# Linear attention and a gated feed-forward layer on one core: attention of the next batch placed in pieces between the feed-forward matmuls

## Chip, core and metric

The kernel runs on one core of one Trainium2 chip. The core has five engines that run their own instruction streams and wait for each other by semaphores: TensorE (PE in the profile; PEld is its weight loading), VectorE (DVE), ScalarE (ACT), GpSimd (POOL, which here only issues loads and sets up constants) and SyncE (SP, which issues the stores). The metric is the device time of one execution in microseconds (us); lower is better.

## What is computed

Eight batches with 8 heads each, a sequence of 1024 and a head dimension of 64. K and V are first projected along the sequence to 64 rows by two fixed matrices E and F, so each head's score matrix is only 1024 x 64. The result of all heads, 8192 tokens of 512 features, goes through a feed-forward layer of width 1536 with a sigmoid gate.

```python
k_proj = np.einsum('ks,bhsd->bhkd', E, k)
v_proj = np.einsum('ks,bhsd->bhkd', F, v)
scores = scale * np.matmul(q, k_proj.transpose(0, 1, 3, 2))
scores = scores - np.max(scores, axis=-1, keepdims=True)
attn = np.exp(scores)
attn = attn / (np.sum(attn, axis=-1, keepdims=True) + 1e-09)
x = np.matmul(attn, v_proj)            # then heads side by side: (8192, 512)
gate = 1.0 / (1.0 + np.exp(-(x @ w_gate)))
val = x @ w_val
out = gate * val @ w_out
```

All inputs and the output are float32 in memory; loads convert to bfloat16 on the way, and the matmuls run in bfloat16 with float32 sums.

## The kernel before

The kernel has two stages, one after the other, with an instruction stream written out by hand for each engine (`pool_prog`, `dve_prog`, `pe_prog`, `act_prog`, `sync_prog`).

**Attention.** The loop runs over 32 pairs of heads (`NPAIR`, four per batch). For a pair, PE does these steps: `P1` projects K (L284) and V (L296), 16 matmuls of 64 columns each, the two heads on the two column halves of the PE array (`tile_position` (0, 0) and (0, 64)), so that their results stand in the upper and lower 64 partitions. `P2` transposes Q (L320, 16 transposes of 128 columns, in blocks of eight, first one head and then the other). `P34` makes the scores with the sequence on the partitions (L340). ACT takes the exponential (L524); no maximum is subtracted. DVE sums it along the 64 columns (L214), takes the reciprocal (L221) and multiplies (L226, `softmax_pair`). `P5` transposes the weights back (L357), DVE copies them out of PSUM (L204, L207), and `P6` multiplies by the projected V (L382). ACT copies the result to `xT` (L507, L511), which holds the feed-forward input of all batches, and does the copies of the transposed Q (L495, L498) and of the projections (L487). PE's order around a pair is P34(g), P5(g-1), P2(g+1), P1(g+1), P6(g-1).

**Feed-forward.** After all pairs, PE waits for the last `xT` and then runs over 16 blocks of 512 tokens. A block has 12 steps (`m`, 128 features of the inner width each): four matmuls for the gate (L454), four for the value (L465), each 128x128 by 512 columns. ACT takes the sigmoid of the gate out of PSUM (L541), DVE multiplies it by the value, also out of PSUM (L257), into `hT`. Gate and value banks and the sigmoid buffers are double. After the steps of a block come the output projections of the block before, `emit_outproj`: four tiles of 128 tokens, 12 matmuls each (L430). DVE copies each tile out (L245), SP stores it (L557) from one of two buffers.

**Loads.** POOL issues, in this order: E and F, then for each batch K, V and Q (L163, L166, L169) into two sets of buffers; the gate and value weights in three pieces each (L174, L177) come behind the loads of batch 5, the output weights (L180) last. From batch 2 on the issue waits until PE has read the buffers of two batches earlier. All these loads run in one DMA queue.

DVE's first operations make an identity matrix from two index tables (L188, L189, L191).

Of the kernel before, what the change touches and what calls it, by code (L numbers as in the profile page):

```python
# [6 lines left out]
AF = mybir.ActivationFunctionType  # L7
ALU = mybir.AluOpType
AX = mybir.AxisListType
# [4 lines left out]
P = 128  # L14
S = 1024
# [7 lines left out]
NSLOT = 2  # L23


def bass_linformer_attn__then__ffn_glu_sigmoid_kernel(
# [14 lines left out]
    assert H * DH == DM and H % 2 == 0  # L41
    NPAIR = B * (H // 2)
    PPB = H // 2
    NBLK = B * 2
    NTOT = NBLK * 4
    SCALE = 1.0 / (DH ** 0.5)

    with contextlib.ExitStack() as es:
        _cnt = [0]

        def sbuf(shape, dtype, name="sb"):
            _cnt[0] += 1
            return es.enter_context(nc.sbuf_tensor(f"{name}{_cnt[0]}", shape, dtype))

        def psum(shape, name="ps"):
            _cnt[0] += 1
            return es.enter_context(nc.psum_tensor(f"{name}{_cnt[0]}", shape, FP32))

        def sem():
            _cnt[0] += 1  # L60
            return es.enter_context(nc.semaphore(f"sem{_cnt[0]}"))

        iota_c_i = sbuf([P, P], I32)
        iota_r_i = sbuf([P, 1], I32)
        iota_c = sbuf([P, P], FP32)
        iota_r = sbuf([P, 1], FP32)
        ident = sbuf([P, P], BF16)
        Ebf = sbuf([KPJ, S], BF16)
        Fbf = sbuf([KPJ, S], BF16)
        Eperm = sbuf([KPJ, NT, P], BF16)  # L70
        Fperm = sbuf([KPJ, NT, P], BF16)
        ETp = sbuf([P, NT, KPJ], BF16)
        FTp = sbuf([P, NT, KPJ], BF16)

        Qb = [sbuf([P, H, NT * DH], BF16) for _ in range(NSLOT)]
        Kb = [sbuf([P, H, NT * DH], BF16) for _ in range(NSLOT)]
        Vb = [sbuf([P, H, NT * DH], BF16) for _ in range(NSLOT)]

        qTp = [sbuf([P, S], BF16) for _ in range(2)]
        kpvpSB = [sbuf([P, 128], BF16) for _ in range(3)]  # L80
        attnTp = [sbuf([P, S], BF16) for _ in range(2)]
        expb = [sbuf([P, 2, NT, KPJ], BF16) for _ in range(2)]
        attnN = [sbuf([P, 2, NT, KPJ], BF16) for _ in range(2)]
        rsb = [sbuf([P, 2 * NT], FP32) for _ in range(2)]
        rdb = [sbuf([P, 2 * NT], FP32) for _ in range(2)]

        xT = sbuf([P, NI, B * S], BF16)

        wG = sbuf([P, NI, DFF], BF16)
        wV = sbuf([P, NI, DFF], BF16)  # L90
        wO = sbuf([P, NF, DM], BF16)
        sig = [sbuf([P, 512], BF16) for _ in range(2)]
        hT = [sbuf([P, NF, 512], BF16) for _ in range(2)]
        ostage = [sbuf([P, DM], FP32) for _ in range(2)]

        pkv = psum([P, 512])
        pqbank = psum([P, 512])
        po1 = psum([P, 512])
        psc = [psum([P, 512]) for _ in range(2)]
        patbank = [psum([P, 512]) for _ in range(2)]  # L100
        po0 = psum([P, 512])
        pq = pqbank[:, :].bitcast(BF16)
        pat = [patbank[i][:, :].bitcast(BF16) for i in range(2)]
        pG = [pkv[:, 0:512], pqbank[:, 0:512]]
        pV = [po1[:, 0:512], psc[0][:, 0:512]]
        pO = [psc[1][:, 0:512], po0[:, 0:512]]

        sem_ef = sem()
        sem_q = [sem() for _ in range(NSLOT)]
        sem_k = [sem() for _ in range(NSLOT)]  # L110
        sem_v = [sem() for _ in range(NSLOT)]
        NWCH = 3
        sem_wg = [sem() for _ in range(NWCH)]
        sem_wv = [sem() for _ in range(NWCH)]
        sem_wo = sem()
        sem_out = [sem(), sem()]
        sem_init_iota = sem()
        sem_init_perm = sem()
        sem_init_pe = sem()
        sem_init_act = sem()  # L120
        sem_pe_kpvp = sem()
        sem_pe_qT = sem()
        sem_pe_scores = sem()
        sem_pe_trans = sem()
        sem_pe_out = sem()
        sem_act_qT = sem()
        sem_act_exp = sem()
        sem_act_xT = sem()
        sem_act_kpvp = sem()
        sem_dve_red = sem()  # L130
        sem_dve_rcp = sem()
        sem_dve_norm = sem()
        sem_dve_attnT = sem()
        sem_pe_gate = sem()
        sem_pe_val = sem()
        sem_pe_proj = sem()
        sem_act_sig = sem()
        sem_dve_h = sem()
        sem_dve_oevac = sem()

        out_v = out[:, :].rearrange("(x y) c -> y x c", y=NT)

        with nc.Block() as block:

            def pool_prog(gp):
                gp.iota(iota_c_i[:, :], [[1, P]], channel_multiplier=0)
                gp.iota(iota_r_i[:, :], [[1, 1]], channel_multiplier=1).then_inc(
                    sem_init_iota, 1
                )
                gp.dma_start(Ebf[:, :], E[:, :]).then_inc(sem_ef, 16)  # L150
                gp.dma_start(Fbf[:, :], F[:, :]).then_inc(sem_ef, 16)
                CW = DFF // NWCH
                wg_v = moe_w_gate.rearrange("(i p) f -> p i f", p=P)
# [439 lines left out]
```

## Time and profile before

| | us |
|---|---|
| median of 3 runs | 689.93 (689.55 to 691.05) |
| profiled execution, first to last instruction | 687.5 |
| first matmul of the attention stage on the projections | 17.85 |
| first weight load of the feed-forward stage | 185.53 |

The profiled execution has 2.4 us less span than the median of the timed runs: the span leaves out what lies before the first instruction and after the last. A group's row gives busy time, the mean duration of one instruction in ns, and the idle time of the engine just before with what ended it. Matmul durations hold the way through the array, so that those of a row of matmuls overlap; the rate is read from the starts. "PEclk" is the granted clock of TensorE as a share of full speed. A chain of waits goes back from the last instruction to what released each step.

### The profile page before, as it was taken

How to read it: one execution, taken by the hardware profiler on the slowest of the kernel's cores; microseconds unless marked ns; L12 is line 12 of the kernel's file. 1: busy time of each engine (PE TensorE's matmuls, PEld its weight loads, DVE VectorE, ACT ScalarE, POOL GpSimd, SP SyncE). 2: the span in 40 equal slices, each digit the busy share in tenths (PEclk: the TensorE clock that was granted, in tenths of full speed). 3: DMA queues.
4: the chain of work that ended last, by engine and by line, in shares of the span. 5: the costliest groups of instructions: out<-in, count | busy, mean ns of one | idle time of the engine just before them, and what ended most of it. 6: DMA issues, size and time to landing. Idle time of an engine off the chain costs nothing.

```text
span 687.5 us, 11735 instructions
## 1 busy us (share of the span) xinstructions
PE 603.9 (88%) x4961; PEld 311.4 (45%) x5008; DVE 286.7 (42%) x421; ACT 221.8 (32%) x420; POOL 29.1 (4%) x39
## 2 busy tenths in 40 slices
PE   0676666367599999999999999999999999999998
PEld 0555555255344444444444444444444444444443
DVE  1377777537433343433333343433333333334332
ACT  1377777357433131312212131312222131312220
POOL 4011141200000000000000000000000000000000
PEclk9999999779899999999999999999999999999999
DMA  9999999996000101010100101010100101010102
GB/s 143 207 165 177 184 176 207 207 207 102 2 0 1 51 11 62 0 62 15 47 31 31 47 17 61 1 61 1 62 31 33 47 15 62 1 61 1 61 16 107
DMA packets 39107, 47.67 MB, mean 69 GB/s; under 512 B 1552, under 2 KB 30736, under 8 KB 39056
## 3 DMA queue, kind: packets, MB, share of 16 engines
q0 software_dynamic: 29840, 30.15, 27.0%
q1 hardware_dynamic: 9216, 16.78, 6.5%
q8 instruction: 39, 0.64, 0.4%
q14 instruction: 12, 0.10, 0.0%
HBM read 60.29 MB, written 16.78 MB: 112 GB/s over the span
## 4 chain that ended last, share of the span: by engine, by line
PE 77%; DVE 11%; DMA 10%; issue 1%; POOL 1%; ACT 1%; POOLq 0%
PE ps L454 24%; PE ps L465 24%; PE ps L430 24%; DMA sb<-in_q_dram 10%; DVE sb L226 4%; DVE sb L214 4%; PE ps L357 3%; DVE sb L204 1%; DVE sb L207 1%; DVE sb L221 1%; PE ps L320 1%; POOL sb L163 0%; POOL sb L166 0%; PE ps L382 0%; PE ps L340 0%
## 5 line engine op out<-in xcount | busy, mean ns | idle before, releaser
L541 ACT ACTIVATE sb<-ps 128x512 bf16<-128x512 f32 x192 | 114.6, 597 | 361.9 <-PE ps L454 361.9
L257 DVE TENSOR_TENSOR sb<-sb,ps 128x512 bf16<-128x512 bf16 x192 | 132.1, 688 | 204.3 <-PE ps L465 204.3
L454 PE MATMUL ps<-sb 128*128 128x512 bf16 x751 | 195.6, 380 | 2.0 <-ACT sb L511 1.2
L465 PE MATMUL ps<-sb 128*128 128x512 bf16 x754 | 195.7, 380 | 0.7
L430 PE MATMUL ps<-sb 128*128 128x512 bf16 x752 | 167.2, 379 | 0.8
L454 PEld LDWEIGHTS ps<-sb 128*128 128x128 bf16 x768 | 75.2, 98 | 92.3 <-ACT sb L511 1.6
L465 PEld LDWEIGHTS ps<-sb 128*128 128x128 bf16 x768 | 75.4, 98 | 91.2 <-issue 1.1
L430 PEld LDWEIGHTS ps<-sb 128*128 128x128 bf16 x768 | 75.1, 98 | 90.6
L245 DVE COPY sb<-ps 128x512 f32<-128x512 f32 x64 | 44.3, 692 | 120.8 <-PE ps L430 118.6
L357 PE MATMUL ps<-sb 128*64 128x128 bf16 x512 | 30.2, 231 | 31.9 <-DVE sb L226 31.9
L214 DVE TENSOR_REDUCE sb<-sb 128x16 f32<-128x1024 bf16 x32 | 38.7, 1209 | 20.1 <-ACT sb L524 20.1
L320 PE MATMUL ps<-sb 128*64 128x128 bf16 x512 | 31.2, 235 | 16.3 <-DMA sb<-in_q_dram 16.3
L357 PEld LDWEIGHTS ps<-sb 128*64 128x64 bf16 x512 | 24.8, 115 | 36.1 <-DVE sb L226 36.0
L495 ACT ACTIVATE sb<-ps 128x512 bf16<-128x512 bf16 x32 | 19.1, 597 | 64.4 <-PE ps L320 64.4
L226 DVE TENSOR_TENSOR sb<-sb 128x1024 bf16<-128x1024 bf16 x32 | 39.2, 1225 | 1.1
L524 ACT ACTIVATE sb<-ps 128x512 bf16<-128x512 f32 x64 | 36.1, 646 | 1.5 <-PE ps L340 1.5
L320 PEld LDWEIGHTS ps<-sb 128*64 128x64 bf16 x512 | 25.7, 118 | 16.7 <-DMA sb<-in_q_dram 16.6
L204 DVE COPY sb<-ps 128x512 bf16<-128x512 bf16 x32 | 13.6, 424 | 46.4 <-PE ps L357 46.4
L284 PE MATMUL ps<-sb 128*64 128x64 bf16 x512 | 21.7, 203 | 9.4 <-DMA sb<-in_v_dram 9.4
L340 PE MATMUL ps<-sb 64*128 64x64 bf16 x512 | 18.5, 194 | 10.1 <-ACT sb L498 8.5
L340 PEld LDWEIGHTS ps<-sb 64*128 64x128 bf16 x512 | 15.0, 97 | 25.1 <-ACT sb L498 24.5
L382 PE MATMUL ps<-sb 64*64 64x512 bf16 x128 | 21.1, 411 | 1.7 <-DVE sb L207 1.7
(37 smaller groups left out, 187.4 us busy)
## 6 DMA issues: line engine op xcount, KB each, us to landing
out_dram<-sb SPq DMA_DIRECT2D x64, 256.0 KB, 2.0
sb<-in_k_dram POOLq DMA_DIRECT2D x8, 1024.0 KB, 9.7
sb<-in_v_dram POOLq DMA_DIRECT2D x8, 1024.0 KB, 14.2
sb<-in_q_dram POOLq DMA_DIRECT2D x8, 1024.0 KB, 18.3
sb<-in_moe_w_gate_dram POOLq DMA_DIRECT2D x3, 512.0 KB, 23.4
sb<-in_moe_w_val_dram POOLq DMA_DIRECT2D x3, 512.0 KB, 25.2
sb<-in_moe_w_out_dram POOLq DMA_DIRECT2D x1, 1536.0 KB, 36.5
sb<-in_E_dram POOLq DMA_DIRECT2D x1, 128.0 KB, 3.0
```

What stands on the lines that cost most here:

```text
L214: dv.tensor_reduce(rsb[ps][:, :], expb[ps][:, :, :, :].rearrange("p h t k -> p (h t) k"), AX.X, ALU.add,).then_inc(sem_dve_red, 1)
L226: dv.tensor_tensor(attnN[ps][:, :, :, :].rearrange("p h t k -> p (h t) k"), expb[ps][:, :, :, :].rearrange("p h t k -> p (h t) k"), bcast, ...
L245: dv.tensor_copy(ostage[T % 2][:, :], pO[T % 2][:, 0:512]).then_inc(sem_dve_oevac, 1)
L257: dv.tensor_tensor(hT[hslot][:, m, :], sig[M % 2][:, :], pV[M % 2][:, 0:512], ALU.mult).then_inc(sem_dve_h, 1)
L320: last = te.matmul(pq[ho : ho + 64, t * P : (t + 1) * P], Qb[sb][:, h, t * DH : (t + 1) * DH], ident[:, :], is_transpose=True, tile_positi ...
L340: last = te.matmul(psc[hl][:, t * KPJ : (t + 1) * KPJ], qTp[sp][ho : ho + 64, t * P : (t + 1) * P], kpvpSB[skv][ho : ho + 64, 0:64], tile_ ...
L357: last = te.matmul(pat[sa][ho : ho + 64, t * P : (t + 1) * P], attnN[sa][:, hl, t, :], ident[:, :], is_transpose=True, tile_position=(0, ho),)
L430: last = te.matmul(pO[T % 2][:, 0:512], hT[hslot][:, m, tt * P : (tt + 1) * P], wO[:, m, :], start=(m == 0), stop=(m == NF - 1),)
L454: last = te.matmul(pG[M % 2][:, 0:512], wG[:, i, m * P : (m + 1) * P], xT[:, i, c0 : c0 + 512], start=(i == 0), stop=(i == NI - 1),)
L465: last = te.matmul(pV[M % 2][:, 0:512], wV[:, i, m * P : (m + 1) * P], xT[:, i, c0 : c0 + 512], start=(i == 0), stop=(i == NI - 1),)
L524: ac.activation(expb[ps][:, hl, :, :].rearrange("p t k -> p (t k)"), psc[hl][:, :], AF.Exp, scale=SCALE,).then_inc(sem_act_exp, 1)
L541: ac.activation(sig[M % 2][:, :], pG[M % 2][:, 0:512], AF.Sigmoid).then_inc(sem_act_sig, 1)
```

## The change

The order of all work is now written by one program that records operations (`Plan.add`) with the data that each reads (`r`), writes (`w`) or holds alone (`x`, a PSUM bank), and then emits each engine's stream in the recorded order with the waits that follow (`Plan.emit`). There is one counting semaphore per engine; every operation on which another one depends increments its own engine's.

Attention of batch 0 runs first, alone. Then, for each batch b, the 24 feed-forward steps and the output tiles of the blocks before them form a list of slots (`slots`), 32 per batch (28 in the first), and the 25 pieces of attention of batch b+1 are placed between the slots, at most one behind each. An output tile follows every third step. `xT` has two buffers of one batch in place of one for all. Three PSUM banks (`PA`) serve attention in turn, two each serve gate and value, one the output tiles.

Attention itself changes. The projections (`kv`) run for four head pairs at once, 256 columns, the two column halves in turn; the projected K is transposed (`kt`) into a block-diagonal matrix of 128x128 per head pair (`kpBD`), and V is copied into another (`vpBD`). Q is transposed with the heads in turn (`qt`). Scores (`sc`) come out transposed: the 64 projected rows of both heads on the partitions, 512 tokens as columns. The exponential goes straight to `eT`, and its sums over the partitions are matmuls with a matrix of ones and zeros, four 32-column tiles in turn (`den`). DVE takes the reciprocal in four pieces of 128 columns (`rec`), splits it into a bfloat16 part and its remainder (`split`), one matmul with a selecting matrix spreads it over the partitions (`bc`), DVE multiplies, and one matmul per head pair and half sequence gives `xT` (`xo`).

The sigmoid becomes a hyperbolic tangent of half the gate; DVE adds one and multiplies by the value in one operation, and the factor of one half is applied where an output tile is copied out. The tangent is kept in float32, in three buffers; there are four output buffers.

The loads stand in the order E, F, K, V, Q of batch 0, the six gate and value pieces, K, V, Q of batch 1, the output weights, then batches 2 to 7. POOL also fills the constant matrices: four wide and sixteen small memsets and one more index table, between the loads of batch 0 and those of the weights. From the diff (helpers and constants cut; `...` where lines are left out):

```diff
-                for g in range(NPAIR + 1):
-                    if g < NPAIR:
-                        P34(g)
-                    if g >= 1:
-                        P5(g - 1)
-                    if g + 1 < NPAIR:
-                        P2(g + 1)
-                        P1(g + 1)
-                    if g >= 1:
-                        P6(g - 1)
-                te.wait_ge(sem_act_xT, 2 * NPAIR)
-                te.wait_ge(sem_act_kpvp, NPAIR)
-                te.wait_ge(sem_dve_attnT, 2 * NPAIR)
...
-                    ac.activation(sig[M % 2][:, :], pG[M % 2][:, 0:512], AF.Sigmoid).then_inc(
...
+class Plan:
...
+    def add(self, eng, fn, r=(), w=(), x=(), dma=None):
...
+        def dep(o, raw):
+            if o is op:
+                return
+            if o.eng == eng and o.dma is None:
+                if eng == "PE" or (eng != "POOL" and not raw):
+                    return
+            deps[id(o)] = o
...
+        for k in tuple(w) + tuple(x):
+            for o in self.writers.get(k, ()):
+                dep(o, False)
+            for o in self.readers.get(k, ()):
+                dep(o, False)
...
+                for op in mine:
+                    want = {}
+                    for o in op.deps:
+                        want[o.sem] = max(want.get(o.sem, 0), o.val)
+                    for s, v in want.items():
+                        if seen.get(s, 0) < v:
+                            e.wait_ge(sem(s), v)
+                            seen[s] = v
+                    inst = op.fn(e)
...
+        bank = [
+            es.enter_context(nc.psum_tensor(n, [P, 512], FP32))
+            for n in ("pG0", "pG1", "pV0", "pV1", "pO", "pA0", "pA1", "pA2")
+        ]
+        PG, PV, PO, PA = (0, 1), (2, 3), 4, (5, 6, 7)
...
+        def mm(b, o, lhsT, rhs, r, start=True, stop=True, tp=None, tr=False):
...
+                kw["start"], kw["stop"] = start, stop
+            return add("PE", lambda e: e.matmul(o, lhsT, rhs, **kw), r=r, x=[("bank", b)])
+        def act(o, i, r, w, b=None, func=AF.Copy, scale=1.0):
+            x = [] if b is None else [("bank", b)]
+            return add("ACT", lambda e: e.activation(o, i, func, scale=scale), r=r, w=w, x=x)
...
+        def next_bank():
+            b = PA[turn[0] % 3]
+            turn[0] += 1
+            return b
+        def attention(b):
+            s = b % 2
+            st = {}
+            def kv():
+                bk = next_bank()
+                for src, wt, c0, n in ((Kb[s], ET, 0, "K"), (Vb[s], FT, 256, "V")):
+                    sv = src[:, :, :].rearrange("p (r h) (t d) -> p h t r d", h=2, t=NT)
+                    for t in range(NT):
+                        for h in range(2):
+                            mm(
+                                bk,
+                                bank[bk][64 * h : 64 * h + 64, c0 : c0 + 256],
+                                wt[:, t, :],
+                                sv[:, h, t, :, :],
+                                [(n, s), ("ET" if n == "K" else "FT")],
                                 start=(t == 0),
                                 stop=(t == NT - 1),
+                                tp=(0, 64 * h),
                             )
+                act(kp[:, :, :], bank[bk][:, 0:256], [], ["kp"], b=bk)
+                for h in range(2):
+                    hh = slice(64 * h, 64 * h + 64)
+                    act(
+                        vpBD[hh, :, hh],
+                        bank[bk][hh, 256:512].rearrange("p (r d) -> p r d", r=NR),
+                        [],
+                        [f"vpBD{h}"],
+                        b=bk,
+                    )
+            def kt():
+                bk = next_bank()
+                ob = bank[bk][:, :].bitcast(BF16)
+                for r in range(NR):
+                    for h in range(2):
+                        mm(
+                            bk,
+                            ob[64 * h : 64 * h + 64, r * P : (r + 1) * P],
+                            kp[:, r, :],
+                            ident[:, :],
+                            ["kp", "ident"],
+                            tr=True,
+                            tp=(0, 64 * h),
+                        )
+                for h in range(2):
+                    hh = slice(64 * h, 64 * h + 64)
+                    act(
+                        kpBD[hh, :, hh],
+                        ob[hh, 0:512].rearrange("p (r c) -> p r c", r=NR)[:, :, hh],
+                        [],
+                        [f"kpBD{h}"],
+                        b=bk,
+                    )
+            def qt(r):
+                bk = next_bank()
+                ob = bank[bk][:, :].bitcast(BF16)
                 for t in range(NT):
+                    for h in range(2):
+                        mm(
+                            bk,
+                            ob[64 * h : 64 * h + 64, t * P : (t + 1) * P],
+                            Qb[s][:, 2 * r + h, t * DH : (t + 1) * DH],
+                            ident[:, :],
+                            [("Q", s), "ident"],
+                            tr=True,
+                            tp=(0, 64 * h),
+                        )
+                dve(lambda e: e.tensor_copy(qT[:, r, :], ob[:, :]), [], [("qT", r)], b=bk)
+            def sc(r):
+                for hf in range(2):
+                    bk = next_bank()
+                    mm(
+                        bk,
+                        bank[bk][:, :],
+                        kpBD[:, r, :],
+                        qT[:, r, hf * 512 : (hf + 1) * 512],
+                        ["kpBD0", "kpBD1", ("qT", r)],
                     )
+                    act(
+                        eT[:, r, hf, :],
+                        bank[bk][:, :],
+                        [],
+                        [("eT", r, hf)],
+                        b=bk,
+                        func=AF.Exp,
+                        scale=SCALE,
                     )
+            def den():
+                bk = next_bank()
+                st["den"] = bk
+                for rnd in range(2):
+                    for j in range(4):
+                        r, hf = 2 * rnd + j // 2, j % 2
+                        mm(
+                            bk,
+                            bank[bk][32 * j : 32 * j + 32, :],
+                            dsel[:, rnd, :],
+                            eT[:, r, hf, :],
+                            ["dsel", ("eT", r, hf)],
+                            start=(rnd == 0),
+                            stop=(rnd == 1),
+                            tp=(0, 32 * j),
+                        )
+            def rec(c):
+                bk = st["den"]
+                cc = slice(c * 128, (c + 1) * 128)
+                dve(
+                    lambda e: e.reciprocal(rden[:, cc], bank[bk][:, cc]),
+                    [],
+                    [("rden", c)],
+                    b=bk,
+                )
+            def split():
+                rd = [("rden", c) for c in range(4)]
+                dve(lambda e: e.tensor_copy(rhi[:, :], rden[:, :]), rd, ["rhi"])
+                dve(
+                    lambda e: e.scalar_tensor_tensor(
+                        rhl[:, :], rhi[:, :], negm[:, 0:1], rden[:, :], ALU.mult, ALU.add
+                    ),
+                    rd + ["rhi", "negm"],
+                    ["rhl"],
+                )
+            def bc(c):
+                r, hf = c // 2, c % 2
+                rnd, j = r // 2, 2 * (r % 2) + hf
+                bk = next_bank()
+                mm(bk, bank[bk][:, :], bsel[:, j, rnd, :], rhl[:, :], ["bsel", "rhl"])
+                dve(
+                    lambda e: e.tensor_tensor(
+                        aT[c % 2][:, :], eT[:, r, hf, :], bank[bk][:, :], ALU.mult
+                    ),
+                    [("eT", r, hf)],
+                    [("aT", c % 2)],
+                    b=bk,
+                )
+            def xo(c):
+                r, hf = c // 2, c % 2
+                bk = next_bank()
+                mm(
+                    bk,
+                    bank[bk][:, :],
+                    vpBD[:, r, :],
+                    aT[c % 2][:, :],
+                    ["vpBD0", "vpBD1", ("aT", c % 2)],
+                )
+                act(
+                    xT[s][:, r, hf * 512 : (hf + 1) * 512],
+                    bank[bk][:, :],
+                    [],
+                    [("xT", s, r, hf)],
+                    b=bk,
+                )
+            out = [kv, lambda: qt(0), kt, lambda: qt(1)]
+            out += [lambda: sc(0), lambda: qt(2), lambda: sc(1), lambda: qt(3)]
+            out += [lambda: sc(2), lambda: sc(3), den]
+            out += [lambda c=c: rec(c) for c in range(4)] + [split]
+            out += [lambda: bc(0)]
+            for c in range(1, 8):
+                out += [lambda c=c: (bc(c), xo(c - 1))]
+            out += [lambda: xo(7)]
+            return out
+        def mstep(blk, m):
+            s, hf = (blk // 2) % 2, blk % 2
+            M = blk * NF + m
+            j = m // (NF // NWCH)
+            for W, pb, n in ((wG, PG[M % 2], "wG"), (wV, PV[M % 2], "wV")):
+                for i in range(NI):
+                    mm(
+                        pb,
+                        bank[pb][:, :],
+                        W[:, i, m * P : (m + 1) * P],
+                        xT[s][:, i, hf * 512 : (hf + 1) * 512],
+                        [(n, j), ("xT", s, i, hf)],
+                        start=(i == 0),
+                        stop=(i == NI - 1),
                     )
+            sg = sig[M % 3]
+            act(
+                sg[:, :],
+                bank[PG[M % 2]][:, :],
+                [],
+                [("sig", M % 3)],
+                b=PG[M % 2],
+                func=AF.Tanh,
+                scale=0.5,
+            )
+            dve(
+                lambda e: e.scalar_tensor_tensor(
+                    hT[blk % 2][:, m, :],
+                    sg[:, :],
+                    1.0,
+                    bank[PV[M % 2]][:, :],
+                    ALU.add,
+                    ALU.mult,
+                ),
+                [("sig", M % 3)],
+                [("hT", blk % 2, m)],
+                b=PV[M % 2],
+            )
+        def oproj(blk, tt, pb):
+            T = 4 * blk + tt
+            for m in range(NF):
+                mm(
...
+            o = ost[T % 4]
+            dve(
+                lambda e: e.tensor_scalar(o[:, :], bank[pb][:, :], 0.5, None, op0=ALU.mult),
+                [],
+                [("ost", T % 4)],
+                b=pb,
+            )
...
+        def slots(b):
+            for blk in (2 * b, 2 * b + 1):
+                for m in range(NF):
+                    yield lambda blk=blk, m=m: mstep(blk, m)
+                    if m % 3 == 2 and blk >= 1:
+                        yield lambda blk=blk, m=m: oproj(blk - 1, m // 3, PO)
+        constants()
+        project_consts()
+        for j in range(NWCH):
+            load_w(j)
+        for piece in attention(0):
+            piece()
+        load_kvq(1)
+        load(wO[:, :, :], moe_w_out.rearrange("(m p) c -> p m c", p=P), ["wO"], "wO")
+        for b in range(B):
...
+            pieces = attention(b + 1) if b + 1 < B else []
+            todo = list(slots(b))
+            n, done = len(todo) - 1, 0
+            for i, slot in enumerate(todo):
+                slot()
+                while done < len(pieces) and done * n < (i + 1) * len(pieces):
+                    pieces[done]()
+                    done += 1
...
+            if load_next is not None:
+                load_kvq(load_next)
+        last = 2 * B - 1
+        for tt in range(4):
+            oproj(last, tt, ((PO,) + PA)[tt])
+        plan.emit(nc, es, final=[f"out{i}" for i in range(4)])
```

693 lines of the change are left out of this document (235 added, 458 removed).

## The prediction

> **What bounds the kernel now.** I read the page's first two parts, the chain of work that ended last, a table by stage, and then single stretches.
>
> ```profile
> span 687.5 us, 11735 instructions
> ...
> PE   0676666367599999999999999999999999999998
> ...
> DMA  9999999996000101010100101010100101010102
> ```
>
> The last two rows cut the span into 40 slices of 17.2 us, a digit for each slice's busy share in tenths. There are two stages: ten slices with busy DMA and a half-busy PE (attention), then thirty with PE full and the DMA almost idle (feed-forward). The table by stage (columns: stretch, length, busy time of PE, PEld, DVE, ACT, POOL, granted clock, DMA share, GB/s):
>
> ```profile
> 93.00:142.00 49.00, 25.92 (x693) 20.55 (x690) 30.22 (x45) 25.72 (x56) 11.48 (x14) 0.88 1.23 203
> 142.00:182.00 40.00, 27.55 (x681) 21.64 (x680) 26.87 (x40) 26.91 (x58) 0.00 (x0) 0.93 0.66 110
> 182.00:190.00 8.00, 6.00 (x31) 2.64 (x28) 1.45 (x3) 3.34 (x5) 0.00 (x0) 0.61 0.01 2
> 190.00:687.50 497.50, 491.86 (x2245) 223.87 (x2288) 175.62 (x255) 113.66 (x191) 0.00 (x0) 1.00 0.09 34
> ```
>
> After 190 us PE is the whole bound: DVE is busy for 176 of 497 us, ACT for 114. Before 182 us no engine is full: in the chain of waits the same DVE line returns in almost every period, with two long stretches of waiting for a load.
>
> ```profile
> 4.34 18.42 DMA sb<-in_q_dram
> ...
> 82.51 1.24 DVE sb L226
> 86.92 1.24 DVE sb L226
> 92.84 48.55 DMA sb<-in_q_dram x2
> ```
>
> One pair of heads takes 86.92 - 82.51 = 4.41 us (L214, L221, L226 and the copies in turn), and 48.55 us are a wait for loads queued behind the weights. So some 185 us go by before feed-forward begins, and PE could have done feed-forward work in most of them. The steady rate, from PE's timeline:
>
> ```profile
> 471.74 1.03 PE L454 MATMUL ps<-sb 128*128 128x512 bf16 x4
> 472.60 1.03 PE L465 MATMUL ps<-sb 128*128 128x512 bf16 x4
> 473.47 1.03 PE L454 MATMUL ps<-sb 128*128 128x512 bf16 x4
> ```
>
> Eight matmuls in 473.47 - 471.74 = 1.73 us: 0.216 us each, whatever the 1.03 of a group says (it holds the last one's latency).
>
> **The change, part by part.** Prices first, from the groups by line (busy us, mean ns, idle before):
>
> ```profile
> L541 ACT ACTIVATE sb<-ps 128x512 bf16<-128x512 f32 x192 | 114.6, 597 | 361.9 <-PE ps L454 361.9
> L257 DVE TENSOR_TENSOR sb<-sb,ps 128x512 bf16<-128x512 bf16 x192 | 132.1, 688 | 204.3 <-PE ps L465 204.3
> L454 PE MATMUL ps<-sb 128*128 128x512 bf16 x751 | 195.6, 380 | 2.0 <-ACT sb L511 1.2
> ```
>
> ```profile
> L204 DVE COPY sb<-ps 128x512 bf16<-128x512 bf16 x32 | 13.6, 424 | 46.4 <-PE ps L357 46.4
> ```
>
> ```profile
> L221 DVE RECIPROCAL sb<-sb 128x16 f32<-128x16 f32 x32 | 8.1, 253 | 1.1
> ```
>
> ```profile
> L189 DVE CAST sb<-sb 128x1 f32<-128x1 int32 x1 | 0.1, 144 | 0.0
> ```
>
> (1) *Feed-forward matmuls.* 192 steps of 8 and 64 output tiles of 12 remain: 2304 x 0.216 = 498 us. This term does not move.
>
> (2) *The start.* Nothing of batch 1 can run before its K, V and Q have landed, and they are queued behind batch 0 and the six gate and value pieces:
>
> ```profile
> sb<-in_q_dram POOLq DMA_DIRECT2D x8, 1024.0 KB, 18.3
> sb<-in_moe_w_gate_dram POOLq DMA_DIRECT2D x3, 512.0 KB, 23.4
> ```
>
> The columns are issues, size of one and us to landing; K and V are as large as Q, the value pieces as the gate's. Q of batch 0 lands at 4.34 + 18.42 = 22.8 us. Behind it come 6 x 512 KB and 3 x 1024 KB, 6.29 MB; at the 203 GB/s of the 93 to 142 row that is 31.0 us: Q of batch 1 lands at about 53.8 us (V at 48.6). Attention of batch 0, alone at the front, is on my estimate done at 43: from 22.8 us some 8 us of transposes, copies and scores, then 12 us of DVE work (below). One step (up to 3 us at a cold clock), the projections of batch 1 (after 48.6) and a second step fit in before 53.8. So I put the clock to 53.8 us with two steps and one projection piece done. POOL also has 21 new small instructions between the issues of Q and of the weights, which the trace does not show. From nothing to L257's 0.69 us each (a full-width operation) they take up to 14 us, of the 18 that the queue needs for Q after its issue at 4.34; nearest is L189, a tiny one, 0.14: 3 us, hidden. Above 0.88 each they would push everything back. The output weights (1.57 MB, 8 us more) are wanted only in the third step of block 1, some 20 us later. Later batches load with a whole batch (some 70 us) to spare.
>
> (3) *Attention's PE work inside the feed-forward.* The new projections, transposes and sums are column-tiled. What such matmuls cost is in the steady attention stage:
>
> ```profile
> 150.52 0.72 PE L357 MATMUL ps<-sb 128*64 128x128 bf16 x13 [0.98 <-DVE sb L226]
> 151.03 0.24 PE L320 MATMUL ps<-sb 128*64 128x128 bf16 x1
> ...
> 151.54 0.22 PE L284 MATMUL ps<-sb 128*64 128x64 bf16 x1
> ...
> 151.70 0.22 PE L320 MATMUL ps<-sb 128*64 128x128 bf16 x1
> ...
> 152.00 0.48 PE L296 MATMUL ps<-sb 128*64 128x64 bf16 x13
> 152.40 0.62 PE L382 MATMUL ps<-sb 64*64 64x512 bf16 x4
> ```
>
> L357 and L320 start in turn, on different column halves: the halves run at the same time. 32 transposes take 151.70 - 150.52 plus a last one, 1.2 us: 37 ns each, 75 ns within one half. The 32 matmuls of 64 columns that follow run from 151.54 to the last start at 152.28 (152.48 less the 0.20 of one): 24 ns each, 48 in one half. A half thus costs 21 ns plus 0.42 ns a column: 128 ns at 256 columns. The four of L382 in 0.62 us, against 4 x 0.216 = 0.86, show the same for 512 columns. Per batch: qt 64 x 37 = 2.4 us; kt 8 x 37 = 0.3; kv 16 x 128 = 2.05; den two rounds of four at 0.22 = 0.45; sc, bc and xo 24 x 0.216 = 5.2. Together 10.4.
>
> Entering and leaving a column-tiled piece: L296's last start at 152.28 and L382 at 152.40 lie 0.12 apart where 0.024 were due: 0.1 for a change of tiling. From 0 to one matmul's latency beyond its pitch, 0.380 - 0.216 = 0.164 (L454). I take 0.1; kv, kt, den and four qt make 14 changes: 1.4 us. Then bc(0), which stands one step behind split: DVE ends that step's product 0.7 us after it, the copy and the fused subtract take about 1.3 (unknown here; between 0.25 and 0.69 each by L221 and L257), so rhl comes at 2.0 where the next step ends at 1.73: 0.3. Sum 12.1 us per batch, seven batches 85; less the projections already counted, 83.
>
> (4) *What must stay hidden.* The reciprocal: 16 columns 253 ns against 144 for a one-column operation, 7.3 ns a column; 128 columns cost 1.07 us (between 0.25, if the columns were free, and 2.0, in proportion). DVE per batch: 24 products at 0.69 (L257), 8 output tiles at the same, 4 copies of twice L204's columns at 0.85, 4 reciprocals at 1.07, 1.3 for split, 8 at 0.69: 36 us of PE's 24 x 1.73 + 8 x 2.59 + 12 = 74. ACT: 40 x 0.60 (L541) and small copies, 27. The tightest piece is a reciprocal beside a step, 0.69 + 1.07 = 1.76 in 1.73; every fourth slot is an output tile of 2.59, so nothing piles up. On ACT two exps hold back one tanh by 1.2 us in a slot of 2.16, and the gate bank has a whole step to spare. The tanh and the added one cost what sigmoid and product did; the doubled inputs are undone in L245's place. All this I cost at nothing; with the cover gone it is the third rival.
>
> (5) *The end.* After the last matmul the old tail stays, its last copy and store:
>
> ```profile
> 684.32 0.69 DVE L245 COPY sb<-ps 128x512 f32<-128x512 f32 x1 [1.90 <-PE ps L430]
> ```
>
> 687.5 - 684.3 = 3.2 us.
>
> **Sum**, against the profiled execution: 53.8 + (2304 - 16) x 0.216 = 494.2, + 83 + 3.2 + 1 for a cold clock after the wait for Q = 635.2 us of span. The median before is 689.93 where the span is 687.5; with the same 2.4 us around it, 637.6, say **638 us**, 7.5% faster. Attention's own 185 us become 54 in front and 83 inside.
>
> **Rivals.** *Column halves one after another.* If the alternating matmuls do not overlap, per batch qt takes 4.8, kt 0.6, kv 4.1 and den 1.8: 6.1 us more, 7 x 6.1 - 2 = 41, **679 us**. The overlap at 151 us speaks against it, though there the halves come in blocks of eight. Chance 0.07.
>
> *A clock that falls back.* After the wait at 182 to 190 us the granted clock was 0.61 and the first step was slow:
>
> ```profile
> 185.53 0.13 PEld L454 LDWEIGHTS ps<-sb 128*128 128x128 bf16 x2 [1.63 <-ACT sb L511]
> ...
> 188.57 0.81 PE L454 MATMUL ps<-sb 128*128 128x512 bf16 x3
> ```
>
> 3.0 us from its first weight load to the next step, against 1.73: 1.3 lost. If each of the 35 transposing pieces (kt and qt, 7 batches) did that, +45: **683 us**. Against it: a piece lasts 0.6 us between steps that keep PE full. The 0.93 of the transposing stage does not decide it. The Trainium skill, "TensorE: Matmul & The Clock Gate", Part 4, says that transposes do not count as a busy PE the way matmuls do; its Part 1 lets the clock drop only after some 3.4 us of idleness. By the first alone this rival would come, by both together not. Chance 0.04.
>
> *Waits between pieces (the slower side).* Each engine works in order, so one late copy on DVE or ACT holds PE and every step behind it. In attention before, such a wait was
>
> ```profile
> PE ps L357 <- DVE sb L226: 31.9, 31, 2.0
> ```
>
> 31.9 / 31 = 1.03 us. Some 14 of 25 pieces per batch (kt, sc, den, bc and xo) read what DVE or ACT made one or two pieces ago: 98 pieces, 101 us, **739 us**. It decides against the change from 0.53 us a piece (the 52 us of gain over 98). Against it: a step of 1.73 us lies between, and part 4 fits within it. Chance 0.06.
>
> *Tables on ACT.* Sigmoid needed a table load of its own:
>
> ```profile
> L541 ACT ACT_TABLE_LOAD x1 | 1.3, 1283 | 0.0
> ```
>
> If exp and tanh too were of different sets, each of 28 score pieces would carry two, 2.57 us: 0 to 72 us. ACT would do 0.60 + 1.20 + 2.57 + 0.60 = 5.0 us in two steps with their pieces, 4.5 us of PE, so most stays hidden; I take 20, **658 us**. No row shows where tanh belongs. The Trainium skill, "ScalarE: Activation LUTs", Table sets, lists tanh in the set of exp, by which this costs nothing. Chance 0.05.
>
> **Chances and range.** The forecast holds 0.78. Its own range: with no cost for the changes of tiling and no wait at bc(0), 12 us less, **624**; with 0.164 a change (+6), weights 3 us late and 4 us of small waits, 651. The tables case carries it to **664**; beyond lie the serial halves, the clock and the waits, 0.17, and half of the tables. Faster by over 0.2% (what a measurement of this kernel can tell from none): all but the waits and the worst of the tables, 0.91; within it 0.02; slower 0.07.
>
> **What would show it.** PE's row of slices full from the fourth on; the first feed-forward step at 43 to 47 us, a gap before Q of batch 1 lands at 54; steps still 1.73 us apart; about 10 to 12 us of PE between them per batch; one table load in all. Wrong if the first steps come after 60 us, if tanh is preceded by loads, or if PE waits for DVE or ACT for more than 0.5 us at a piece.

## The result and the profile after

| | before | after |
|---|---|---|
| median, us | 689.74 (689.49 to 691.05) | 629.19 (628.78 to 630.13) |
| ratio, 95% interval | | 0.912 (0.9107 to 0.9133) |
| profiled execution, span, us | 687.5 | 627.3 |

The change takes 8.8% off, 60.5 us; the forecast was 52. Page of the kernel after, the slices of the span:

```profile
span 627.3 us, 8171 instructions
...
PE   2558999999999999999999999999999999999997
...
PEclk9978999999999999999999999999999999999999
DMA  9999990652009500375006620000000000000002
```

There is one stage now. PE is full from the fifth slice on (62.7 us), the granted clock stays at nine tenths or more, and the loads of later batches come in bursts that nothing waits for. The chain that ended last says the same, by line (all matmuls have the line of one helper, L202, so the PSUM banks tell them apart: pG gate, pV value, pO output, pA attention):

```profile
PE pG L202 26%; PE pO L202 25%; PE pV L202 25%; PE pA L202 12%; DMA Qb<-in_q_dram 6%; DVE ost L563 1%; DVE aT L471 1%; ACT sig L206 1%; POOL wG L221 0%; POOL dsel L258 0%; POOL wV L221 0%; POOL Kb L221 0%; POOL Vb L221 0%; POOL bsel L251 0%; POOL Qb L221 0%
```

Before, 77% of the chain was PE, 11% DVE and 10% DMA; now 88% is PE, and most of what is left belongs to the first 54 us. Behind them PE waits for another engine at two places only, 0.4 us for DVE in the first batch (at 88, shown below) and 0.9 us for an output copy at 612.6. The long pieces of the chain in order of time (start, length) repeat with the batch:

```profile
275.92 2.54 PE pO L202 x11
...
349.03 2.54 PE pO L202 x11
...
422.14 2.54 PE pO L202 x11
```

A batch takes 349.03 - 275.92 = 422.14 - 349.03 = 73.11 us. Its 24 steps and 8 output tiles are 288 matmuls at 0.216 us, 62.2 us; attention of the next batch takes the other 10.9. The table by stage for one such period (length, busy time of PE, PEld, DVE, ACT, POOL, clock, DMA share, GB/s):

```profile
119.99:193.10 73.11, 72.48 (x417) 33.91 (x426) 33.85 (x51) 25.27 (x45) 2.63 (x3) 1.00 0.37 72
```

PE 72.5 of 73.1 us (some records are missing), DVE 34, ACT 25: the forecast had 74, 36 and 27.

### The profile page after: what moved, and what is told of

It is laid out like the page before. It is cut to its first block, busy times and chain, and to the rows that moved or that the text cites. A ratio compares the mean times of both kernels' runs of the same rounds, so it can differ in the third digit from the quotient of the medians.

```text
span 627.3 us, 8171 instructions
## 1 busy us (share of the span) xinstructions
PE 589.8 (94%) x3344; PEld 274.7 (44%) x3408; DVE 275.8 (44%) x413; ACT 204.5 (33%) x363; POOL 32.4 (5%) x60
## 4 chain that ended last, share of the span: by engine, by line
PE 88%; DMA 6%; POOL 2%; DVE 2%; issue 1%; ACT 1%; DVEq 0%; POOLq 0%
PE pG L202 26%; PE pO L202 25%; PE pV L202 25%; PE pA L202 12%; DMA Qb<-in_q_dram 6%; DVE ost L563 1%; DVE aT L471 1%; ACT sig L206 1%; POOL wG L221 0%; POOL dsel L258 0%; POOL wV L221 0%; POOL Kb L221 0%; POOL Vb L221 0%; POOL bsel L251 0%; POOL Qb L221 0%
## 5 line engine op out<-in xcount | busy, mean ns | idle before, releaser
L536 DVE SCALAR_TENSOR_TENSOR hT<-sig,pV 128x512 bf16<-128x512 f32 x192 | 132.1, 688 | 211.4 <-PE pV L202 207.2
L202 PE MATMUL pG<-xT,wG 128*128 128x512 bf16 x750 | 195.4, 380 | 2.2 <-issue 1.4
L202 PE MATMUL pV<-xT,wV 128*128 128x512 bf16 x746 | 195.7, 380 | 0.8
L206 ACT ACTIVATE sig<-pG 128x512 f32<-128x512 f32 x192 | 114.8, 598 | 246.1 <-PE pG L202 231.7
L202 PE MATMUL pO<-wO,hT 128*128 128x512 bf16 x717 | 166.1, 379 | 2.3 <-issue 1.0
L202 PEld LDWEIGHTS pV<-xT,wV 128*128 128x128 bf16 x768 | 75.4, 98 | 91.2 <-issue 1.1
L202 PEld LDWEIGHTS pG<-xT,wG 128*128 128x128 bf16 x768 | 72.2, 98 | 88.2 <-issue 4.4
L202 PEld LDWEIGHTS pO<-wO,hT 128*128 128x128 bf16 x732 | 70.6, 98 | 85.8 <-DVE ost L563 1.3
L563 DVE TENSOR_SCALAR ost<-pO 128x512 f32<-128x512 f32 x61 | 42.2, 692 | 104.4 <-PE pO L202 104.4
L471 DVE TENSOR_TENSOR aT<-eT,pA 128x512 bf16<-128x512 bf16 x64 | 43.5, 681 | 2.1 <-PE pA L202 2.0
L202 PE MATMUL pA<-rhl,bsel 128*128 128x512 bf16 x58 | 23.0, 400 | 6.2 <-DVE rhl L458 5.0
L202 PE MATMUL pA<-ident,Qb 128*64 128x128 bf16 x512 | 21.5, 229 | 4.3 <-DMA Qb<-in_q_dram 4.0
L202 PE MATMUL pA<-aT,vpBD 128*128 128x512 bf16 x63 | 24.4, 387 | 0.8 <-DVE aT L471 0.7
L202 PEld LDWEIGHTS pA<-ident,Qb 128*64 128x64 bf16 x512 | 16.2, 114 | 18.4 <-issue 11.4
L202 PE MATMUL pA<-qT,kpBD 128*128 128x512 bf16 x63 | 19.1, 384 | 0.8 <-ACT kpBD L206 0.5
L202 PE MATMUL pA<-Kb,ET 128*64 128x256 bf16 x128 | 9.4, 294 | 6.7 <-DMA Kb<-in_k_dram 6.7
L202 PE MATMUL pA<-Vb,FT 128*64 128x256 bf16 x128 | 9.2, 292 | 5.5 <-DMA Vb<-in_v_dram 5.5
```

The source lines that it names most:

```text
L202: return add("PE", lambda e: e.matmul(o, lhsT, rhs, **kw), r=r, x=[("bank", b)])
L206: return add("ACT", lambda e: e.activation(o, i, func, scale=scale), r=r, w=w, x=x)
L471: lambda e: e.tensor_tensor(aT[c % 2][:, :], eT[:, r, hf, :], bank[bk][:, :], ALU.mult),
L536: lambda e: e.scalar_tensor_tensor(hT[blk % 2][:, m, :], sg[:, :], 1.0, bank[PV[M % 2]][:, :], ALU.add, ALU.mult,),
L563: lambda e: e.tensor_scalar(o[:, :], bank[pb][:, :], 0.5, None, op0=ALU.mult),
```

## Where the first 54 us go

PE's timeline of the kernel after, from the first feed-forward step on:

```profile
43.76 1.02 PE L202 MATMUL pG<-xT,wG 128*128 128x512 bf16 x4
44.62 1.03 PE L202 MATMUL pV<-xT,wV 128*128 128x512 bf16 x4
45.58 1.06 PE L202 MATMUL pA<-Kb,ET 128*64 128x256 bf16 x16
48.94 1.06 PE L202 MATMUL pA<-Vb,FT 128*64 128x256 bf16 x16 [2.30 <-DMA Vb<-in_v_dram]
50.16 1.30 PE L202 MATMUL pG<-xT,wG 128*128 128x512 bf16 x3 [0.16 <-issue]
51.25 1.91 PE L202 MATMUL pV<-xT,wV 128*128 128x512 bf16 x4
54.00 0.64 PE L202 MATMUL pA<-ident,Qb 128*64 128x128 bf16 x16 [0.83 <-DMA Qb<-in_q_dram]
54.57 1.04 PE L202 MATMUL pG<-xT,wG 128*128 128x512 bf16 x4
```

The first step stands at 43.76 (forecast 43), PE waits for V of batch 1 until 48.94 (48.6), and for Q until 54.00 (53.8). In the bracket is the idle time just before and what ended it. The second step, behind the wait for V, takes about 3.0 us instead of 1.73 (from 49.9 to 53.0; the record of its first matmul is missing). The granted clock of that stretch is 0.57. This only shortens the wait for Q.

## The experiments

Theory: after the landing of Q of batch 1 the time is the sum of PE's work, one matmul behind the other, and DVE, ACT and the loads are hidden. Rivals: the new form of attention is the gain and not its place; the column halves overlap no better, or no worse, in another order; table loads, or DVE's work, reach PE through waits. Spans of profiled executions are compared with the 627.3 us of the kernel after; ratios are to the kernel before on the same chip.

**1. The pieces behind the slots instead of between them.**

```diff
                 slot()
-                while done < len(pieces) and done * n < (i + 1) * len(pieces):
-                    pieces[done]()
-                    done += 1
             while done < len(pieces):
```

> All 25 pieces of the next batch stand behind the batch's last slot instead of between its slots; every instruction stays. If the gain is the placement: alone, a batch's attention takes about 21 us from its Q on (22.6 to 43.8 us at the front of the changed kernel), 10.9 of which PE needs in any place; 7 x (21 + about 1 for kv - 10.9) = 78 us more, less some 5 us of waiting for the loads of batch 1 at the front: about 700 us, slower than the kernel before the change (689.7). If the new form of attention is the gain and its place matters little: below 650 us.

Measured: 704.31 us, ratio 1.020 (1.0185 to 1.022), span 701.9. PE's timeline at the end of the first batch's slots:

```profile
92.69 2.75 PE L202 MATMUL pO<-wO,hT 128*128 128x512 bf16 x12
95.37 1.06 PE L202 MATMUL pA<-Kb,ET 128*64 128x256 bf16 x16
...
109.79 1.04 PE L202 MATMUL pA<-rhl,bsel 128*128 128x512 bf16 x2 [4.73 <-DVE rhl L458]
...
117.44 0.38 PE L202 MATMUL pA<-aT,vpBD 128*128 128x512 bf16 x1 [0.49 <-DVE aT L471]
117.66 1.02 PE L202 MATMUL pG<-xT,wG 128*128 128x512 bf16 x4
```

Attention alone holds PE from 95.28 (the end of the output tile, 92.69 + 12 x 0.216) to 117.66, 22.4 us, 4.73 of them in one wait for the reciprocals and the split; the granted clock of the stretch is 0.85. Between the slots the same instructions cost 10.9. Seven times 11.5 is 80 us; the span grew by 74.6. Most of the other 6 is the start of the kernel after, where the waits for batch 1's loads and the slow step make 10.8 us (43.76 to 54.57) of two steps, kv and one qt, which take 6.1 elsewhere. So the placement is worth more than the whole gain. The new form of attention on its own is no gain: 22.4 us a batch in a row, where the old stage took four pairs at 4.41, 17.6 us. What the old form would have given between the slots was not run.

**2. Column halves in blocks.** kv, kt and qt issue one half and then the other (here qt; kv and kt likewise).

```diff
-                for t in range(NT):
-                    for h in range(2):
+                for h in range(2):
+                    for t in range(NT):
                         mm(
                             bk,
                             ob[64 * h : 64 * h + 64, t * P : (t + 1) * P],
```

> kv, kt and qt issue one column half's matmuls as a block and then the other's, as the kernel before did, instead of in turn. If the order is what made the pieces cheaper than forecast (28 ns a transpose in the trace after, 37 forecast from blocks before): qt 0.67 to about 0.8 us, kv 1.98 to 2.25 or more, about 1 us a batch, 7 us in all: 636 us. If blocks inside one piece do not overlap at all, because PE looks too little ahead: qt 0.67 to 1.1 or more, kv to 3.7, kt to 0.65, about 3.7 us a batch: 655 us. If the order does not matter and the forecast was off for another reason: 629 us.

Measured: 639.62 us, ratio 0.926 (0.9248 to 0.9276), span 637.7. A qt piece between two steps in the kernel after, and then with blocks (PE's timeline):

```profile
206.47 1.03 PE L202 MATMUL pV<-xT,wV 128*128 128x512 bf16 x4
207.43 0.64 PE L202 MATMUL pA<-ident,Qb 128*64 128x128 bf16 x16
208.00 1.04 PE L202 MATMUL pG<-xT,wG 128*128 128x512 bf16 x4
```

```profile
267.23 1.03 PE L202 MATMUL pV<-xT,wV 128*128 128x512 bf16 x4
268.19 0.89 PE L202 MATMUL pA<-ident,Qb 128*64 128x128 bf16 x16
269.01 1.04 PE L202 MATMUL pG<-xT,wG 128*128 128x512 bf16 x4
```

The step's last four matmuls take 0.864 us, so the piece costs 208.00 - 207.33 = 0.67 in turn and 269.01 - 268.09 = 0.92 in blocks. In the first 16 transposes start over 0.64 less the 0.22 of one: 28 ns each, 56 ns within a half, about what 128 columns take at 0.42 ns. That leaves no time for the weight loads, whose records there last 114 ns on average; that it is they which the order hides is argued from this, not shown by itself. In blocks it is (0.89 - 0.22) / 15 = 45 ns. The kv pieces, in turn and then in blocks:

```profile
258.74 1.03 PE L202 MATMUL pV<-xT,wV 128*128 128x512 bf16 x4
259.69 1.06 PE L202 MATMUL pA<-Kb,ET 128*64 128x256 bf16 x16
260.59 1.04 PE L202 MATMUL pA<-Vb,FT 128*64 128x256 bf16 x16
261.79 0.81 PE L202 MATMUL pG<-xT,wG 128*128 128x512 bf16 x3 [0.16 <-issue]
262.44 1.03 PE L202 MATMUL pV<-xT,wV 128*128 128x512 bf16 x4
```

```profile
263.01 1.03 PE L202 MATMUL pV<-xT,wV 128*128 128x512 bf16 x4
263.97 1.20 PE L202 MATMUL pA<-Kb,ET 128*64 128x256 bf16 x13
...
266.36 1.04 PE L202 MATMUL pG<-xT,wG 128*128 128x512 bf16 x4
```

1.98 us (259.60 to 261.58, a record of the first gate matmul is missing: the value follows at 262.44) against 266.36 - 263.87 = 2.49. A batch pays 4 x 0.25 + 0.51 = 1.5 us for blocks, seven batches 10.6; the span grew by 10.4. The order matters, and somewhat more than expected (7). Full loss of overlap (655) is out.

**3. Sigmoid again.** The gate goes through the sigmoid, with nothing added and no factor of one half.

```diff
-                func=AF.Tanh,
-                scale=0.5,
+                func=AF.Sigmoid,
+                scale=1.0,
```

> The gate goes through Sigmoid again (scale 1, nothing added, no factor of one half), with the attention pieces where they are. 58 or so loads of 1.28 us appear on ACT. The forecast's view of a covered ACT (26 us of 73 a batch): most stays hidden, between 629 and 649 us. If ACT's order makes PE wait for every pair of loads: 629 + 28 x 2.57 = 701 us.

Measured: 633.60 us, ratio 0.9177 (0.9149 to 0.9206), span 630.1. The group of loads (count, busy us, mean ns, idle before), and a period:

```profile
L206 ACT ACT_TABLE_LOAD x58 | 74.4, 1283 | 1.9 <-PEq L627 0.8
```

```profile
122.77:195.88 73.11, 73.11 (x426) 33.89 (x426) 33.72 (x51) 35.38 (x53) 2.62 (x3) 1.00 0.37 73
```

ACT has 35.4 us of work in the period instead of 25.3, and the period is 73.11 as before: eight loads a batch cost nothing. What shows of the 2.8 us is in the first batch, where block 0 has no output tiles between its steps (PE's timeline):

```profile
74.67 0.61 PE L202 MATMUL pA<-eT,dsel 128*32 128x512 bf16 x6
76.93 0.88 PE L202 MATMUL pA<-eT,dsel 128*32 128x512 bf16 x2 [1.65 <-ACT eT L206]
77.74 1.04 PE L202 MATMUL pG<-xT,wG 128*128 128x512 bf16 x4
```

There the sums wait for the last two exps, and the piece takes 77.74 - 74.57 = 3.2 us instead of 0.65. Two of the four runs, which were not profiled, took 635.1 and 635.7 us, so that the medians lie 4.4 apart; where these two lose 3 us more, no trace shows. So the tangent, by itself, is worth some 3 to 6 us here, not 20 and not 72.

**4. Reciprocals twice.** The first copy goes into a buffer that nothing reads.

```diff
+                dve(
+                    lambda e: e.reciprocal(rscr[:, cc], bank[bk][:, cc]),
+                    [("rscr", c)],
+                    [("rscr", c)],
+                    b=bk,
+                )
```

> Each of the four reciprocals of a batch is made twice (once into a buffer that nothing reads): 3.4 us more of DVE per batch. If DVE is covered: at the front the extra 3.4 us vanish in the wait for Q of batch 1, inside the feed-forward they vanish beside the steps; 629 us, at most 631. If waits between pieces pass DVE's time on to PE: up to 7 x 3.4 = 24 us, 653 us.

Measured: 632.42 us, ratio 0.916 (0.9146 to 0.9174), span 630.4. PE's timeline at the piece after split:

```profile
302.55 2.75 PE L203 MATMUL pO<-wO,hT 128*128 128x512 bf16 x12
305.67 0.39 PE L203 MATMUL pA<-rhl,bsel 128*128 128x512 bf16 x1 [0.37 <-DVE rhl L465]
```

The output tile ends at 302.55 + 2.59 = 305.14, and bc(0) starts at 305.67: 0.53 us of wait, in six of seven batches. In the slots of batch 0 no output tile but a step stands ahead of bc(0); there the wait is 0.84 us, where the kernel after has 0.41 already. Together that is 3.6 us more; the span grew by 3.1, since in this run Q of batch 1 came 0.6 us earlier (its transposes start at 53.41). At the front the added work is hidden in the wait for Q, as expected. So 3.4 us more of DVE a batch become 0.5 of PE, in one place. This is the forecast's wait at bc(0), which the kernel after has in one batch only: behind an output tile there is room for about 2.9 us of DVE, no more, and behind a step there is none. The expectation (631 at most) was missed by the size of this one wait; the rival (653) is far off.

**5. Loads of batch 1 ahead of the later weights.**

```diff
-        for j in range(NWCH):
-            load_w(j)
+        load_w(0)
+        load_kvq(1)
+        load_w(1)
+        load_w(2)
...
-        load_kvq(1)
```

> K, V and Q of batch 1 are loaded behind the first gate and value pieces instead of behind all six; nothing else moves. If the start is set by Q of batch 1 landing at 54.0 us, with 5.4 us of work done by then since 43.8: its wait goes (it lands at about 43), the second step no longer runs at a cold clock, and the time falls by about 5 us, to 624 us. If the start is set by the attention of batch 0 and the transfers are hidden anyway: 629 us. If the second and third weight pieces, now later (48 and 53 us), hold up steps 4 and 8: slower than 624.

Measured: 624.64 us, ratio 0.9036 (0.9023 to 0.9049), span 622.7, 4.6 less than after. The transposes of batch 1's Q, 54.00 in the kernel after, in PE's timeline now:

```profile
48.40 1.03 PE L202 MATMUL pV<-xT,wV 128*128 128x512 bf16 x4
49.35 0.64 PE L202 MATMUL pA<-ident,Qb 128*64 128x128 bf16 x16
```

They follow the second step with no wait, 4.65 us earlier, and all of it is kept. The first step still stands at 43.8.

**6. Transposes together.**

```diff
-            out = [kv, lambda: qt(0), kt, lambda: qt(1)]
-            out += [lambda: sc(0), lambda: qt(2), lambda: sc(1), lambda: qt(3)]
+            out = [kv, lambda: (kt(), qt(0), qt(1))]
+            out += [lambda: sc(0), lambda: (qt(2), qt(3)), lambda: sc(1)]
```

> kt, qt(0) and qt(1) become one piece, qt(2) and qt(3) another: 4 column-tiled pieces per batch instead of 7. If entering and leaving such a piece costs about 0.1 us each way: 3 x 0.21 x 7 = 4.5 us less, 625 us. If a change of tiling costs nothing: 629 us. If three banks filled at once make PE wait for their copies: slower than 629.

Measured: 623.22 us, ratio 0.9022 (0.9007 to 0.9038), span 622.8, 4.5 less than after, as expected. To the tenth this is luck: by the medians the gain is 6.0, and the profiled run is the slowest of its four (spans of 620.9 to 622.8). In it the step behind the wait for Q ran at a granted clock of 0.56 (54.7 to 57.5) and took 1.2 us longer than 1.73. PE's timeline of the doubled qt piece:

```profile
268.43 1.03 PE L202 MATMUL pV<-xT,wV 128*128 128x512 bf16 x4
269.39 1.08 PE L202 MATMUL pA<-ident,Qb 128*64 128x128 bf16 x32
270.40 1.04 PE L202 MATMUL pG<-xT,wG 128*128 128x512 bf16 x4
```

270.40 - 269.29 = 1.11 us for two, against 2 x 0.67: 0.23 us for one entry and exit saved. Three of these are 0.69, and from kv to kv a batch takes 72.43 us (257.87 to 330.30) instead of 73.11. The Trainium skill, "TensorEngine Tiling (Array Packing)", Key Properties, says that a change of the tiling mode drains the array; the trace agrees in so far as each change has a price here, about 0.1 us.

**7 and 8. Q first, and all three.** The loads of batch 1 stand as in experiment 5. For batch 0 alone Q is loaded first, K and V are projected apart, and V comes after the sums.

```diff
+            if b == 0:
+                out = [lambda: qt(0), lambda: qt(1), lambda: qt(2), lambda: kv((0,)), kt]
+                out += [lambda: qt(3)] + [lambda r=r: sc(r) for r in range(4)]
+                out += [den, lambda: kv((1,))]
```

> The load order of e4_loads, and for batch 0 alone Q is loaded first and its pieces stand as Q, K, scores, sums, V. Scores wait for K (17.6 us) instead of Q (22.6). If the chain of batch 0's attention sets the first feed-forward step once the loads of batch 1 no longer do: the first step comes at about 39 us instead of 43.8, 620 us. If the DMA queue still sets the start: no gain over e4_loads.

Measured: 619.57 us, ratio 0.8969 (0.8954 to 0.8984), span 617.7, 5.0 less than with the loads moved alone.

> e4_loads, e7_q_first and e6_transposes_together in one. If the three gains are independent terms of the sum: 629 - 5 - 4.4 - 4.5 = 615 us. If they share the same wait: above 618.

Measured: 614.46 us, ratio 0.8893 (0.888 to 0.8906), span 612.6: 14.7 us less than after, where the three single gains add to 4.6 + 5.0 + 4.5 = 14.1 by the profiled runs and to 4.6 + 5.1 + 6.0 = 15.6 by the medians. The first step (PE's timeline of the kernel with all three):

```profile
38.94 1.02 PE L202 MATMUL pG<-xT,wG 128*128 128x512 bf16 x4
```

It comes at 38.94 instead of 43.76, and no load holds up what follows. So the terms are independent to within 1 us, and this version beats both kernels.

## Why the prediction was right

- **The bound and the sum's form.** Right: start, plus matmuls at 0.216, plus attention's PE time, plus a tail. After: 54.0 + 494.2 + (7 x 10.9 - 2.0) + 3.2 = 625.7, of 627.3 measured; 1.3 of the rest are the two waits of 0.4 and 0.9 us named above. The 1 us of the forecast for a cold clock behind the wait for Q did not come here (the clock is 1.00 from 53.9 to 57.0); in the profiled run of experiment 6 it did. Experiment 1 shows that the placement carries the gain.
- **The start**, 53.8 forecast, 54.0 measured, and for the reason given: experiment 5 moved the loads and took the wait away. That it fits to 0.2 is partly luck: in experiments 2, 3, 4 and 6, with the same order of loads, the transposes of this Q start at 52.6 to 54.2. POOL's 21 small instructions, put at 3 us and bounded at 14, took 5.0 (5.24 to 10.28) and did not show.
- **Attention inside**, 12.1 us a batch forecast, 10.9 measured: this term was mis-sized, by 7 x 1.2 = 8 us, nearly all of the 9 us between 638 and 629. Two steps failed in size. The price of 37 ns a transpose and 128 ns a pair of projections came from a stage that issues the halves in blocks; in turn they cost 28 ns, and 112 (kv's first 16 from 259.69 to 260.59, 8 pairs), together 0.85 us a batch. Experiment 2 put the blocks back and more than that time with them, 1.5 us a batch. And the wait of 0.3 us at bc(0), forecast for every batch, came in one of seven. PE's timeline of the kernel after, in the slots of batch 0 and of batch 3:

```profile
87.06 1.03 PE L202 MATMUL pV<-xT,wV 128*128 128x512 bf16 x4
88.33 0.39 PE L202 MATMUL pA<-rhl,bsel 128*128 128x512 bf16 x1 [0.25 <-DVE rhl L458]
...
301.63 2.75 PE L202 MATMUL pO<-wO,hT 128*128 128x512 bf16 x12
304.44 1.03 PE L202 MATMUL pG<-xT,wG 128*128 128x512 bf16 x4
```

  In the first a step of 1.73 us stands between split and bc(0), as forecast, and PE waits 0.41 us (87.06 + 0.864 to 88.33). In the other six an output tile of 2.59 us stands there: from 301.63 to the next step are 2.81 us, the tile and the one matmul of bc(0), whose record is missing, with nothing between. The forecast took the first case for all. The change of tiling was priced about right (experiment 6).
- **What was to stay hidden** stayed hidden; experiments 3 and 4 say how much room was left: over 10 us of ACT a batch, about 2.9 us of DVE at split where an output tile follows it.
- **The rivals.** Serial halves: no, they overlap in either order. A falling clock: no; in the period above the clock is 1.00 with 72 transposes in five short pieces. The Trainium skill, "TensorE: Matmul & The Clock Gate", Part 4, says that transposes do not count as a busy PE the way matmuls do; by that alone it could have come, and the row decides against it for pieces this short. Waits between pieces: they exist at one place, bc(0), of 0.4 us in one batch, and of 0.5 us in the others when DVE is loaded further (experiment 4). Tables: the kernel after has one load in all.

```profile
L206 ACT ACT_TABLE_LOAD x1 | 1.3, 1283 | 0.8 <-PEq L627 0.8
```

  The Trainium skill, "ScalarE: Activation LUTs", Table sets, lists tanh in the set of exp, and the trace agrees with its one load. Had there been 58, experiment 3 shows 3 to 6 us and not 20.
- **The range.** Its lower end does not follow from its own terms: 12 us off 638 is 626, not 624. Nothing hangs on it here.

## What to carry to other kernels

When one stage is bound by PE and another by chains of short operations on other engines, put the second between the matmuls of the first, one piece a slot: the chain's latency goes and only its PE time stays, 10.9 us of 22.4 here. Then price that PE time from rows with the same order of tiles, and look at what PE cannot start without: here the next batch's loads and the first batch's chain, 10 us that a change of two orders took back. Work on an engine with slack is free up to the tightest slot, so find that slot instead of comparing totals.

## What was not expected of the hardware

Matmuls on the two column halves start closer together when the halves are issued in turn: 128-column transposes at 28 ns each, 45 ns in blocks of eight. The granted clock can fall behind a wait of PE of only 2 us, and not at its end: in the kernel after the wait for V is 2.30 us and ends at 48.94, the clock is 1.00 until 49.9 and 0.50 from 50.4 to 53.1; in experiment 6, behind 1.82 us for Q, it is 0.50 from 54 to 57. With 1.29 and 1.70 us, in experiment 2, it stays at 1.00. On ACT, 1.28 us table loads, 74 us of them, cost 2.8 us of time in the profiled run: ACT is idle for 48 of 73 us of a batch, and the loads lie in there.
